# Lightning attention and a two-layer block on one core: the whole program as one list of steps in another order

## The chip, the cores and the metric

The kernel runs on one core of a Trainium2 chip. The metric is the device time of one execution in microseconds (us), lower is better. A core has five engines that take their instructions from queues of their own, each in order: TensorE (PE; PEld is its weight load), VectorE (DVE), ScalarE (ACT), GpSimd (POOL) and SyncE (SP). They wait for one another through semaphores. Transfers between memory and the chip are issued from POOL, SP or ACT.

## The reference, cut to what matters

```
block = 64                       # B, H, S, D = 4, 8, 768, 64
for b in range(S // block):      # 12 blocks of rows, one after the other
    intra = (qb @ kb.T) * Dmask                     # Dmask: lam ** (i - j), causal
    out   = intra @ vb + (qb * lam_pow) @ kv_state
    kv_state = lam_block * kv_state + (kb * rev_pow).T @ vb
x = out, heads side by side      # 3072 x 512
h = x @ w_in                     # 512 x 2048
g = where(h > 0, h, exp(min(h, 0)) - 1)
result = g @ w_out               # 2048 x 512
```

## The kernel before

The 3072 rows are cut into 24 steps s = 0 to 23. A step holds 64 positions of two batches, 128 rows; steps s and s - 2 belong to the same batches, so the state passes from s - 2 to s. Two steps are one group of 256 rows (groups 0 to 11).

Attention. `visit(so, us, ss, sx)` issues the TensorE work of up to four steps at once: the two matmuls of the output of step `so` (from the state, `I`, and from the scores, `O`), the state update `U` of `us`, the scores `S` of `ss`, and the transposes of q and k of `sx`. Around it stand small words on other engines: `C` copies transposed tiles out of PSUM, `P` multiplies scores by the mask (`att_P`, DVE), `V`, `Q` and `D` are the decays of v, q and state (`vd` line 193, `qs` line 220, `sd` line 211; on DVE or POOL, some `sd` on ACT at line 206), `N` forms the new state (line 281), `X` copies the output into `xt` (ACT). From step 10 on, q and k are transposed by a transfer from SP (`dma_T`, two buffers).

First matmul. A unit (`mm1_h`, line 428) fills one PSUM tile `psH` of 128 x 512 with 8 matmuls over 256 rows or 16 over 128; there are two such tiles. `H group.first column.columns.feature` is a unit of groups 0 to 2, `h group.unit` one of the later groups. Exp and Relu run on ACT (`E`), and one DVE instruction joins them into `g` (`G`). In groups 3 and 4 (its first six units) that join reads copies in SBUF; later it reads `psH` itself (lines 472, 474, 475), so the PSUM tile is free only when `g` is done.

Second matmul. Groups 0 to 2 use `mm2` (`M step.feature`, line 495) and copy the sum out (`Z`). From group 3 on a product of 2 x 2 blocks is formed with seven parts (`part`, line 551) instead of eight; four sums `s` of `g` (line 533, DVE), sums of the weights (`B`), kept partial results (`keep`, ACT) and the final adds and stores (`add`, `c2`, `store`) belong to it.

Loads. POOL issues all loads of k, q, v (12 tiles each) and of the weights: `w_in` in four tiles `wi`, each in two halves, `w_out` in four tiles `wo`. The second half of `wi[2]`, and with it all that is behind it on POOL, waits for the semaphore `crossed`, which TensorE raises at the first visit that reads a state (I2).

Order. The queues follow the order in which the program is written. Before, it comes from three places: a hand-placed start of loads (v0, then k, q, v of step 1, w0, those of 2, w1, those of 3, the first half of w2) and `later_loads()`; a list of words `start` for groups 0 to 2; and then a regular loop over groups 3 to 11 and units 0 to 7, in which a visit stands behind the units 1 and 5, a part of the last group's second matmul behind nearly every unit, and sums, adds, decays and loads at fixed units.

Of the kernel before, what the change touches and what calls it, by code (L numbers as in the profile page):

```python
# [16 lines left out]
def kernel(  # L17
# [41 lines left out]

    NB = 12  # L60
# [23 lines left out]
    def load_step(s):  # L84
        load("k", s)
        load("q", s)
        load("v", s)

# [8 lines left out]
    def load_wi(i, halves=range(2)):  # L97

        for c in halves:
            ins = nc.gpsimd.dma_start(  # L100
                out=wi[i][half(c)],
                in_=moe_w_in[c * DM // 2 : (c + 1) * DM // 2, i * WB : (i + 1) * WB].rearrange(
                    "(g p) f -> p g f", p=64
                ),
            )
            if (i, c) == (2, 1):

                ins.wait_op(crossed, 1, "sem-ge")

    def load_wo(i):  # L110
        nc.gpsimd.dma_start(
            out=wo[i][:],
            in_=moe_w_out[i * WB : (i + 1) * WB, :].rearrange("(g p) f -> p g f", p=128),
        )

# [14 lines left out]
    load("v", 0)  # L130
    load_step(1)
    load_wi(0)
    load_step(2)
    load_wi(1)
    load_step(3)
    load_wi(2, [0])

# [325 lines left out]
    def elu(grp, u):  # L463

        psH, nb, T, name = unit[grp, 0, 2, u]
        if grp == 3 or grp == 4 and u < 6:
            mm1_e(grp, 0, 2, u)
            mm1_g(grp, 0, 2, u, NF2)
            return

        r = msb.tile([128, nb, T], FP32, tag="r", bufs=4, name=f"r{name}")
        nc.scalar.activation(r[:], psH[:], AF.Relu, scale=-1.0)  # L472
        e = msb.tile([128, nb, T], FP32, tag="e", bufs=4, name=f"e{name}")
        nc.scalar.activation(e[:], r[:], AF.Exp, scale=-1.0)  # L474
        nc.vector.scalar_tensor_tensor(  # L475
            out=place(grp, 0, 2, u, 2, NF2), in0=e[:], scalar=-1.0, in1=psH[:],
            op0=ALU.add, op1=ALU.max,
        )

    acc = {}  # L480
    nacc = [0]
# [8 lines left out]
    def mm2(s, n0):  # L490
        if n0 == 0:
            acc[s] = M[nacc[0] % 2][:]
            nacc[0] += 1
# [65 lines left out]
    def part(grp, i):  # L559
        d = res.setdefault(grp, dict(A=M[0], B=M[1]))  # L560
        lo, hi = slice(0, HD), slice(HD, DM)
# [6 lines left out]
    def store(s, o, cols, queues=(nc.sync, nc.sync)):  # L568
        for r in range(2):
            queues[r].dma_start(out=rows(s, r)[:, cols], in_=o[half(r), cols])  # L570
# [16 lines left out]
    def c2(grp, queues=(nc.sync, nc.sync)):  # L587
# [5 lines left out]
        store(2 * grp + 1, d[1], slice(0, DM), queues)  # L593
# [12 lines left out]
    def later_loads():  # L606
        load_wi(2, [1])
        load_wo(0)
        load_wi(3)
        load_wo(1)  # L610
        load_wo(2)
        load("k", 4)
        load("q", 4)
        load_wo(3)
        load("v", 4)
        load_step(5)
        load_step(6)
        load_step(7)
        load_step(8)
        load("k", 9)  # L620
        load("q", 9)
        load("k", 10)
        load("q", 10)
        load("v", 9)
        load("k", 11)
        load("q", 11)
        load("v", 10)

    start = (
        "Fq K0 Fk V0 A...0 C0 A.0.. K1 A..0. P0 A...1 N0 C1 A0... X0 V1 A..1. P1 A.1.. A1... X1 "
        "N1 D2 H0.0.1.0 D3 E0.0.1.0 A...2 V2 C2 Q2 H0.1.1.0 A.2.2. I2 R P2 E0.1.1.0 A2... "
        "G0.0.1.0 H0.0.2.4 X2 N2 H1.0.1.0 E0.0.2.4 D4 G0.1.1.0 A...3 G0.0.2.4 E1.0.1.0 C3 V3 "
        "H1.0.1.4 Q3 E1.0.1.4 H0.0.2.6 A.3.3. I3 P3 G1.0.1.0 E0.0.2.6 H0.0.2.10 A3... E0.0.2.10 "
        "H0.0.2.8 X3 G0.0.2.6 G1.0.1.4 E0.0.2.8 H1.0.1.8 N3 D5 M1.0 G0.0.2.10 G0.0.2.8 E1.0.1.8 "
        "H1.1.1.0 M0.0 E1.1.1.0 G1.0.1.8 B1.0 H1.1.1.4 G1.1.1.0 H0.0.2.14 E1.1.1.4 E0.0.2.14 "
        "G1.1.1.4 G0.0.2.14 H1.1.1.8 M1.4 H0.0.2.12 B1.1 E1.1.1.8 E0.0.2.12 M0.4 H1.0.2.12 "
        "G1.1.1.8 G0.0.2.12 M1.8 E1.0.2.12 A...4 H1.0.2.14 C4 G1.0.2.12 M0.8 E1.0.2.14 Q4 A..4. "
        "G1.0.2.14 M1.12 P4 V4 B2.0 M0.12 Z1 M2.0 Z0 A...5 V5 B4.0 M2.4 C5 M3.0 Q5 B2.1 "  # L640
        "A4.4.5.6 M3.4 P5 X4 N4 H2.0.1.12 C6 H2.0.1.4 E2.0.1.12 Q6 M3.8 D6 B4.1 E2.0.1.4 "
        "H2.0.1.8 G2.0.1.12 V6 M3.12 E2.0.1.8 G2.0.1.4 A5.5.6.7 V7 Z3 G2.0.1.8 H2.0.1.0 X5 N5 "
        "H2.1.1.12 E2.0.1.0 P6 M2.8 D7 E2.1.1.12 G2.0.1.0 H2.1.1.4 M2.12 E2.1.1.4 G2.1.1.12 "
        "H2.1.1.0 C7 Z2 G2.1.1.4 A6.6.7.8 E2.1.1.0 Q7 M4.0 N6 X6 G2.1.1.0 M4.4 P7 H2.1.1.8 C8 "
        "M4.8 E2.1.1.8 V8 D8 Q8 A7.7.8.9 T10 G2.1.1.8 M4.12 X7 N7 P8 Z4 C9 B3.0 B3.1 "
    )
    steps = {
        "I": lambda s: visit(s, None, None, None, True), "C": att_C, "P": att_P, "X": lambda s: att_X(s, nc.scalar),
        "Y": lambda s: att_X(s, nc.vector), "N": att_N, "D": lambda s: decay_s(s, eng=nc.vector), "L": load_step,
        "V": lambda s: decay_v(s, nc.vector if s < 99 else nc.gpsimd),  # L650
        "Q": lambda s: decay_q(s, nc.vector if s < 10 else nc.gpsimd),
        "H": mm1_h, "E": mm1_e, "G": mm1_g, "M": mm2, "Z": mm2_o, "K": consts, "B": w_sum, "T": dma_T,
    }
    for word in start.split():
        if word[0] == "A":
            visit(*(int(x) if x else None for x in word[1:].split(".")))
        elif word[0] == "R":
            later_loads()
        elif word[0] == "F":
            cast0(word[1])  # L660
        else:
            steps[word[0]](*(int(x) for x in word[1:].split(".") if x))

    lo, hi = slice(0, HD), slice(HD, DM)

    five = [(3, 2), (3, 4), (3, 6), (4, 0)]
    nload = 12
    for grp in range(3, NG):  # L670
        old, new = grp - 2, grp - 1
        for u in range(8):
            mm1_h(grp, 0, 2, u, NF2)
            s = 2 * grp + 2 + u // 4
            if s < NS and u % 4 == 0:

                if nload < NS:
                    load("k", nload)
                    load("q", nload)
                if nload <= NS:  # L680
                    load("v", nload - 1)
                    nload += 1
            if s < NS and u % 4 == 1:
                if s not in (10, 12):
                    decay_q(s + 1, nc.vector if s < 10 else nc.gpsimd)
                if s not in (10, 11, 12):
                    decay_s(s + 1, eng=nc.vector if s < 10 else nc.gpsimd)
                visit(
                    s, s if s < NS - NPR else None, s + 1 if s + 1 < NS else None,
                    s + 2 if s + 2 < NT else None,  # L690
                )
                dma_T(s + 3)

            if (grp, u) in five:
                mm2(5, 4 * five.index((grp, u)))
            end = grp == NG - 1
            if old >= 3 and u in (0, 2):
                part(old, {0: 3, 2: 7}[u])
            if new >= 3:
                at_u = {1: 2, 3: 4, 4: 1, 5: 5, 6: 6, 7: 3} if end else {3: 2, 4: 1, 5: 4, 6: 5, 7: 6}  # L700
                if u in at_u:
                    part(new, at_u[u])

            if old >= 3 and u == 1:
                add(old, 0, hi, res[old]["A"][:, hi], "p35")
                store(2 * old, res[old][0], slice(0, DM), ((nc.gpsimd if end else nc.sync),) * 2)
            if old >= 3 and u == 0:
                g_sum(old, 3)
            if new >= 3 and u in (4, 5, 6):
                g_sum(new, {4: 1, 5: 2, 6: 4}[u])  # L710
            if end and u == 3:
                g_sum(new, 3)
            if new >= 3 and u == 4:
                add(new, 0, lo, res[new]["A"][:, hi], "p2")
            if s + 1 < NS:
                if u % 4 == 1:
                    att_P(s + 1)
                if u % 4 == 2:
                    att_C(s + 2)
                    att_N(s)  # L720
                if u in (3, 7) and grp > 3:
                    decay_v(s + 1, nc.vector)
                if (grp, u) == (4, 2):
                    decay_q(s + 1, nc.vector)
            if old >= 3 and u == 2:
                c2(old)
            elu(grp, u)
            if (grp, u) == (5, 3):
                decay_q(s + 1, nc.vector)
            if (grp, u) == (4, 4):  # L730
                decay_s(11)
            if (grp, u) in ((5, 2), (5, 4)):
                decay_s(13, range(2) if u == 2 else range(2, NHP))
# [4 lines left out]
            if (grp, u) == (4, 5):  # L738
                decay_s(12)
# [71 lines left out]
```

## Time and profile before

| | |
|---|---|
| runs | 205.8, 208.4, 208.91 us; median 208.4 |
| profiled execution | 204.2 us from the first to the last instruction; its own whole time is not given apart |
| PE, DVE, ACT, POOL busy | 189.6, 168.7, 146.5, 123.4 us |
| instructions | 7590 |
| bytes moved | 24.36 MB, mean 119 GB/s |

A busy time is the sum over an engine's instructions, those that overlap counted once. In the profile a line such as `L428` is the kernel's line, `out<-in` the tiles, `x16` a count of instructions, and a bracket names how long the engine was idle before an instruction and what released it. A slow release may be put down to a wrong engine where several were waited for.

### The profile page before, as it was taken

What the parts mean: (1) busy time and instruction counts of PE and PEld (TensorE: products, weight loads), DVE (VectorE), ACT (ScalarE), POOL (GpSimd) and SP (SyncE); (2) the same over time, 40 slices, a digit from 0 to 9 for tenths busy, and PEclk for the clock granted to TensorE, in tenths of its full rate; (3) what the DMA queues carried; (4) which work ended last, traced back from release to release, by engine and by line L of the source; (5) the groups of instructions that cost most, each with busy time, mean ns of one, the idle gap of its engine ahead of it and who ended that gap; (6) DMA issues with size and microseconds to landing.
All of it is one profiled execution on the core that took longest, in us unless ns stands there. A gap on an engine that the chain in (4) does not pass through costs nothing.

```text
span 204.2 us, 7590 instructions
## 1 busy us (share of the span) xinstructions
PE 189.6 (93%) x3216; PEld 156.6 (77%) x3216; DVE 168.7 (83%) x279; ACT 146.5 (72%) x283; POOL 123.4 (60%) x174
## 2 busy tenths in 40 slices
PE   0679899999999999999999989999999999999991
PEld 0457777647777777888888878888888888888881
DVE  4776996489989998999989999989979866758672
ACT  5626987635774879999878677788688788876820
POOL 8977832598998959997709999999222200020000
PEclk9999999999999999999999999999999999999998
DMA  6999999999999999999999999999915404004043
GB/s 102 157 171 171 152 206 196 180 124 156 117 148 150 173 108 172 153 134 78 74 163 109 206 105 86 185 111 105 169 27 69 94 0 108 0 6 100 3 103 103
DMA packets 94194, 24.36 MB, mean 119 GB/s; under 512 B 86160, under 2 KB 91152, under 8 KB 94160
## 3 DMA queue, kind: packets, MB, share of 16 engines
q0 software_dynamic: 73744, 13.64, 94.7%
q1 hardware_dynamic: 19968, 9.77, 26.9%
q10 hardware_dynamic: 448, 0.46, 1.0%
q8 instruction: 25, 0.41, 0.9%
q14 instruction: 9, 0.07, 0.1%
HBM read 27.27 MB, written 6.29 MB: 164 GB/s over the span
## 4 chain that ended last, share of the span: by engine, by line
PE 85%; DVE 4%; DMA 3%; POOL 3%; issue 2%; ACT 1%; POOLq 0%; DVEq 0%
PE psH L428 40%; PE psM L551 23%; PE psM L495 10%; DMA wi<-in_moe_w_in_dram 3%; PE psO_None L328 2%; POOL vn L79 1%; PE psZ L352 1%; PE psO_None L337 1%; PE psHB L551 1%; PE psHA L551 1%; DVE s L533 1%; PE psZ L344 1%; DVE g L475 1%; POOL kn L79 1%; PE psO L359 1%
## 5 line engine op out<-in xcount | busy, mean ns | idle before, releaser
L428 PE MATMUL psH<-xt,wi 128*128 128x256 f16 (+1 forms) x896 | 100.1, 261 | 1.9 <-ACT e L438 0.6
L428 PEld LDWEIGHTS <-wi 128*128 128x128 f16 x896 | 78.2, 100 | 13.3 <-issue 2.1
L475 DVE SCALAR_TENSOR_TENSOR g<-e,psH 128x512 f16<-128x512 f32 x58 | 39.6, 683 | 14.3 <-ACT e L474 13.8
L472 ACT ACTIVATE r<-psH 128x512 f32<-128x512 f32 x58 | 34.7, 598 | 18.3 <-PE psH L428 18.2
L474 ACT ACTIVATE e<-r 128x512 f32<-128x512 f32 x58 | 36.5, 630 | 1.8
L79 POOL DMA_DIRECT2D kn<-in_k_dram x46 | 32.2, 720 | 9.2 <-DMA wo<-in_moe_w_out_dram 5.1
L79 POOL DMA_DIRECT2D vn<-in_v_dram x48 | 34.1, 741 | 2.0 <-DMA wi<-in_moe_w_in_dram 1.1
L438 ACT ACTIVATE e<-psH 128x512 f32<-128x512 f32 x38 | 22.8, 601 | 14.7 <-PE psH L428 14.4
L551 PEld LDWEIGHTS <-s 128*128 128x128 f16 x288 | 28.1, 98 | 3.3
L445 DVE SCALAR_TENSOR_TENSOR g<-e,r 128x512 f16<-128x512 f32 x38 | 25.7, 685 | 4.1 <-ACT r L440 4.0
L220 POOL TENSOR_TENSOR qs<-TD,powi 128x512 f16<-128x512 f16 x11 | 13.9, 1264 | 19.3 <-PE psO_None L328 13.1
L79 POOL DMA_DIRECT2D qn<-in_q_dram x36 | 25.3, 735 | 0.0
L551 PE MATMUL psM<-wt,s 128*128 128x256 f16 x192 | 24.9, 273 | 0.0
L495 PE MATMUL psM<-wo,g 128*128 128x512 f16 x96 | 24.0, 379 | 0.0
L440 ACT ACTIVATE r<-psH 128x512 f16<-128x512 f32 x38 | 22.9, 602 | 0.0
L551 PEld LDWEIGHTS <-g 128*128 128x128 f16 x216 | 20.6, 98 | 2.6
L193 DVE TENSOR_TENSOR vd<-vn,rev 128x512 f16<-128x512 f16 x22 | 17.2, 783 | 1.8 <-DMA vn<-in_v_dram 1.7
L228 DVE TENSOR_TENSOR P<-psZ,mask 128x512 f16<-128x512 f32 x24 | 16.4, 684 | 2.0 <-PE psZ L344 1.1
L551 PE MATMUL psM<-wo,g 128*128 128x256 f16 x136 | 17.6, 272 | 0.0
L495 PEld LDWEIGHTS <-g 128*128 128x128 f16 x96 | 8.7, 98 | 7.0
L570 POOL DMA_DIRECT2D out_dram<-o x2 | 1.1, 574 | 21.1 <-DVE o L585 21.1
L533 DVE TENSOR_TENSOR s<-g 128x1024 f16<-128x1024 f16 x18 | 13.8, 764 | 0.0
(85 smaller groups left out, 228.7 us busy)
## 6 DMA issues: line engine op xcount, KB each, us to landing
out_dram<-o SPq DMA_DIRECT2D x43, 128.0 KB, 3.3
vn<-in_v_dram POOLq DMA_DIRECT2D x48, 64.0 KB, 5.0
kn<-in_k_dram POOLq DMA_DIRECT2D x46, 64.0 KB, 4.3
qn<-in_q_dram POOLq DMA_DIRECT2D x36, 64.0 KB, 4.5
wi<-in_moe_w_in_dram POOLq DMA_DIRECT2D x8, 256.0 KB, 8.9
wo<-in_moe_w_out_dram POOLq DMA_DIRECT2D x4, 512.0 KB, 12.6
qn<-in_q_dram POOLq DMA_DIRECT2D x5, 128.0 KB, 5.3
kraw<-in_k_dram SPq DMA_DIRECT2D x2, 128.0 KB, 4.7
```

Of the source, the lines that this page charges most:

```text
L79: nc.gpsimd.dma_start(out=keep[s][half(r)], in_=src[b + r, :, c * L : (c + 1) * L, :].rearrange("h p d -> p h d"),)
L193: eng.tensor_tensor(out=st[s]["vd"][:], in0=vn[s][:], in1=rev[:].unsqueeze(2).broadcast_to([128, H, D]), op=ALU.mult,)
L228: nc.vector.tensor_tensor(out=d["P"][:].rearrange("p y j t -> p y (j t)"), in0=psS, in1=mask[:].rearrange("p y j t -> p y (j t)"), op=ALU. ...
L428: nc.tensor.matmul(psH[:, i, :], lhsT=wi[n // 4][:, kk, (n % 4) * 128 : (n % 4 + 1) * 128], rhs=xt[grp][:, kk, c0 * 128 : c0 * 128 + T], s ...
L438: nc.scalar.activation(e[:], psH[:], AF.Exp)
L440: nc.scalar.activation(r[:], psH[:], AF.Relu)
L445: nc.vector.scalar_tensor_tensor(out=place(grp, c0, nc_, n0, nb, step), in0=e[:], scalar=-1.0, in1=r[:], op0=ALU.add, op1=ALU.min,)
L472: nc.scalar.activation(r[:], psH[:], AF.Relu, scale=-1.0)
L474: nc.scalar.activation(e[:], r[:], AF.Exp, scale=-1.0)
L475: nc.vector.scalar_tensor_tensor(out=place(grp, 0, 2, u, 2, NF2), in0=e[:], scalar=-1.0, in1=psH[:], op0=ALU.add, op1=ALU.max,)
L495: nc.tensor.matmul(acc[s], lhsT=g_of(s, n), rhs=wo[n // 4][:, n % 4, :], start=(n == 0), stop=(n == NFT - 1),)
L551: nc.tensor.matmul(to, lhsT=lhsT, rhs=rhs, start=start and n == 0, stop=stop and n == NF2 - 1, skip_group_check=True,)
```

## The change

The whole order, loads and loop included, becomes one list `plan`, read word by word. `start`, `later_loads()` and the loop are gone; each former loop statement is now a word (`h`, `e`, `g`, `p` part, `s` sum, `k` keep, `a` add, `c`, `o` store, `d` decay on ACT, and a trailing `.1` puts a decay on POOL). Each engine has the same instructions as before, each as often, in another order. The wait on `crossed` before the second half of `wi[2]` is gone. The bank of each of the first six `mm2` sums is a table.

```
+    plan = (
+        "lv1 Fq Fk A...0 C0 A..0. lv0 K0 P0 A0... V1 lq2 lq1 lk1 lk2 w0.0 w0.1 lv2 w1.1 A...1 K1 "
+        "w1.0 lv3 lq3 lk3 V0 C1 A.0.. N0 D2 A...2 w2.1 w2.0 A..1. P1 A.1.. N1 A1... X0 H0.0.1.0 "
+        "X1 C2 y0 w3.1 lq4 Q2 lk4 V2 E0.0.1.0 w3.0 H0.1.1.0 E0.1.1.0 A.2.2. P2 I2 A2... X2 N2 "
+        "G0.0.1.0 H0.0.2.4 H1.0.1.0 A...3 y1 E0.0.2.4 G0.1.1.0 V3 D4 E1.0.1.0 H1.0.1.4 y2 D3 C3 "
+        "H0.0.2.6 Q3 G1.0.1.0 E1.0.1.4 I3 A.3.3. H0.0.2.10 P3 G1.0.1.4 y3 E0.0.2.6 A3... N3 "
+        "G0.0.2.6 G0.0.2.4 E0.0.2.10 H0.0.2.8 lv4 H1.0.1.8 M0.0 G0.0.2.10 X3 H1.1.1.4 E0.0.2.8 "
+        "E1.0.1.8 G1.0.1.8 E1.1.1.4 H1.1.1.8 E1.1.1.8 A...4 H1.1.1.0 lq5 lq6 lk5 E1.1.1.0 "
+        "H0.0.2.14 E0.0.2.14 G0.0.2.8 M1.0 H1.0.2.12 E1.0.2.12 M1.4 H0.0.2.12 G1.1.1.8 D5 "
+        "G0.0.2.14 B1.0 B2.0 E0.0.2.12 G0.0.2.12 C4 H1.0.2.14 lv5 B1.1 G1.1.1.4 M0.4 M1.8 A..4. "
...
+        "G2.1.1.0 h3.3 e3.1 Q9 e3.0 lv10 A8.8.9. lk12 M4.12 e3.4 lq13 D9 T12 N8 g3.1 P9 h3.2 "
+        "lk14 lv12 lk13 V9 lv13 h3.7 e3.3 B4.1 g3.4 Z3 M5.0 g3.0 X8 g3.3 e3.2 A9.9.10. P10 h3.5 "
+        "h3.6 M5.4 Q10 M5.8 N9 e3.7 X9 lq14 h4.3 e3.5 g3.7 V10 e3.6 h4.2 Q11 A10.10.11. Q12.1 "
+        "lk17 lv19 M5.12 T13 h4.0 h4.1 d11.0.4 Z4 g3.2 g3.5 lk15 V11 lk20 lq17 D10 e4.3 e4.2 X10 "
...
+        "g7.6 P18 e7.7 g7.7 k6.p35 a6.0 e8.0 A18.18.19. X18 h8.1 e8.1 p6.7 h8.2 o12.0 P19 s7.1 "
+        "g8.0 p7.2 N18 h8.3 lk21 g8.1 e8.2 A19.19.20. D19.1 h8.4 e8.3 k7.p2 c6 g8.2 p7.1 h8.5 "
...
+        "k10.c45 s10.4 p10.6 e11.6 k10.u2 g11.5 h11.7 p10.3 g11.6 p10.7 a10.2 e11.7 g11.7 o20.0 "
+        "s11.1 j p11.1 p11.4 p11.5 o19.0 o17.0 s11.2 s11.4 s11.3 k11.u1 p11.6 c10 k11.u2 o21.0 "
+        "p11.2 a11.3 o22.1 p11.7 k11.c45 c11 o23.3 p11.3 a11.2 o22.2 "
+    )
...
-    def load_step(s):
...
-    def load_wi(i, halves=range(2)):
-        for c in halves:
-            ins = nc.gpsimd.dma_start(
...
-            if (i, c) == (2, 1):
-                ins.wait_op(crossed, 1, "sem-ge")
+    def load_wi(i, c):
+        nc.gpsimd.dma_start(
...
+    loads = {
+        "l": lambda a: load(a[0], int(a[1:])), "w": lambda a: load_wi(*map(int, a.split("."))),
+        "y": lambda a: load_wo(int(a)),
+    }
...
-    load("v", 0)
-    load_step(1)
-    load_wi(0)
-    load_step(2)
-    load_wi(1)
-    load_step(3)
-    load_wi(2, [0])
...
+    BANK = (1, 0, 0, 1, 0, 1)
...
-    def later_loads():
-        load_wi(2, [1])
-        load_wo(0)
-        load_wi(3)
-        load_wo(1)
-        load_wo(2)
-        load("k", 4)
-        load("q", 4)
-        load_wo(3)
-        load("v", 4)
-        load_step(5)
...
-    for grp in range(3, NG):
-        old, new = grp - 2, grp - 1
-        for u in range(8):
-            mm1_h(grp, 0, 2, u, NF2)
...
+    steps = {
...
+        "K": consts, "B": w_sum, "T": dma_T, "h": lambda g, u: mm1_h(g, 0, 2, u, NF2), "e": elu_e,
+        "g": elu_g, "s": g_sum, "p": part_of, "a": sums, "c": c2, "o": store,
     }
+    for word in plan.split():
...
+        elif word[0] in loads:
+            loads[word[0]](word[1:])
```

## The prediction

> **What bounds the kernel now.** I read the page first, then stretches of the span by engine, then the chain that ended last and the timelines of the places where TensorE stands still.
>
> ```profile
> PE 189.6 (93%) x3216; PEld 156.6 (77%) x3216; DVE 168.7 (83%) x279; ACT 146.5 (72%) x283; POOL 123.4 (60%) x174
> PE 85%; DVE 4%; DMA 3%; POOL 3%; issue 2%; ACT 1%; POOLq 0%; DVEq 0%
> ```
> ```profile
> 0.00:13.24 13.24, 4.64 (x136) 3.51 (x137) 8.34 (x23) 6.93 (x20) 11.15 (x22) 1.00 1.27 138
> 13.24:34.00 20.76, 19.34 (x345) 16.29 (x346) 16.04 (x28) 14.69 (x29) 12.63 (x19) 1.00 1.34 181
> 34.00:112.00 78.00, 78.00 (x1473) 60.33 (x1472) 70.98 (x116) 59.02 (x117) 62.83 (x91) 1.00 1.76 137
> 112.00:126.00 14.00, 13.47 (x236) 11.48 (x235) 13.67 (x20) 10.67 (x20) 14.00 (x18) 1.00 1.52 133
> 126.00:204.20 78.20, 74.11 (x1031) 64.96 (x1029) 59.65 (x97) 55.16 (x100) 22.74 (x27) 0.99 0.63 80
> ```
> The second fence has a stretch, its length, and the busy time of PE, PEld, DVE, ACT and POOL. TensorE is the bound: from 34 to 112 us it never stops, and after 126 only a tail of 4.1 us is missing. It is idle 8.6 us before the first unit of the first matmul (word H), 1.4 us up to 34, 0.5 around 118, and in the tail. The change moves no work to another engine, so it can win only in these four places and lose anywhere.
>
> **The start.** The rows are GpSimd's load issues (start, duration), then the chain from w0 on, then a later H.
>
> ```profile
> 1.41 1.54 POOL L79 DMA_DIRECT2D vn<-in_v_dram  x2 [0.15 <-issue]
> 7.01 0.71 POOL L100 DMA_DIRECT2D wi<-in_moe_w_in_dram  x1 [0.20 <-issue]
> 7.71 1.38 POOL L79 DMA_DIRECT2D kn<-in_k_dram  x2
> 9.05 0.56 POOL L76 DMA_DIRECT2D qn<-in_q_dram  x1
> ```
> ```profile
> 7.01 6.18 DMA wi<-in_moe_w_in_dram
> 13.24 1.89 PE psH L428 x16
> 15.13 0.57 PE psM L398 x9
> 15.70 0.54 PE psM L403 x4
> 16.24 1.71 PE psH L428 x16
> 18.45 0.70 DVE P L228
> ...
> 29.11 0.89 PE psH L428 x16
> ```
> The first H waits for the second half of w0: issued at 7.01, 6.18 us to land, start at 13.24. In the new list k2 and q2 stand ahead of w0, 1.38 + 0.56 = 1.94 us more of issuing, so w0 lands near 15.2. There is a second way to be late. Ahead of H now also stands step 2's transpose (A...2), and k2's second half goes out near 7.7. The next rows are the landing times of k1's loads and of k2's in the old order.
>
> ```profile
> DMA to landing us min/median/max: 4.8/4.9/5.0
> DMA to landing us min/median/max: 5.6/5.8/6.0
> ```
> With 5.0 to 6.0 us, then the transpose (0.54) and S, P and O of step 1 (about 1.5 together), that chain ends between 14.7 and 15.7. I take 15.4 for the first H: +2.2, bounds +1.5 and +3.0. In return step 2's transpose no longer stands between the first two H: 0.57 + 0.54 = -1.1. K0 and V0 now run on VectorE after the first casts instead of in its wait for them; I cost that at nothing, as they end long before k2 lands. If k2 were early it would be 1.2 us of VectorE, and P0 would be late next.
>
> The first two H took 1.89 and 1.71 us, the same 16 matmuls 0.89 us at 29.11. So TensorE begins at half speed and reaches full speed about 4.6 us after it became dense, although the granted clock reads 1.00 there. The sum lets this repeat. The Trainium skill ("TensorE: Matmul & The Clock Gate", part 1) says that the clock opens after a busy window of about 3.4 us and that the windows run free of the kernel's start. The trace agrees with the order of it (4.6 us); by that rule the instant is a matter of phase, and denser work before the first H can open it a window sooner, which is the faster rival.
>
> **The removed wait and the weights.**
>
> ```profile
> 16.69 0.64 POOL L100 DMA_DIRECT2D wi<-in_moe_w_in_dram  x1
> 18.81 0.61 POOL L100 DMA_DIRECT2D wi<-in_moe_w_in_dram  x1 [1.48 <-PE psO_None L328]
> 24.93 1.03 PE L428 MATMUL psH<-xt,wi 128*128 128x256 f16 x8 [0.63 <-ACT e L438]
> 25.12 0.54 POOL L76 DMA_DIRECT2D qn<-in_q_dram  x1 [0.84 <-DMA wi<-in_moe_w_in_dram]
> 32.94 1.05 PE L428 MATMUL psH<-xt,wi 128*128 128x128 f16 x16 [0.30 <-ACT r L440]
> wi<-in_moe_w_in_dram POOLq DMA_DIRECT2D x8, 256.0 KB, 8.9
> wo<-in_moe_w_out_dram POOLq DMA_DIRECT2D x4, 512.0 KB, 12.6
> ```
> The second half of w2 was held 1.48 us for `crossed` and landed 6.2 us after its issue, just before 25.12, where a load that waited for it goes on. H0.0.2.10, its first reader, began at 24.93 after 0.63 idle; the releaser named had long ended, so I read this wait as w2's. In the new list nothing holds w2: behind v3, q3 and k3 its halves go out near 16.6 and 17.5 and land by 24, while the reader comes near 25.5. So -0.6, bounds -0.6 and 0 (the median half of wi took 8.9 us). The units that follow press ScalarE as before, but a transpose (A...4, 0.7 us) now stands among them and gives it that time: the 0.30 goes, -0.3. By the same count w3 and wo1 go out 0.7 and 2.2 us later, w3 near 21.5 and wo1 near 23.6; with 8.9 and 12.6 us they land near 30.4 and 36.2, their readers come near 33 and 35.6: 0, at worst +1.
>
> **The steady part.** A unit's buffer is free again when its g on VectorE is done, and TensorE meets it two units later.
>
> ```profile
> 99.14 0.87 PE psH L428 x8
> 100.70 0.98 PE psM L551 x8
> 93.14 0.60 ACT L472 ACTIVATE r<-psH 128x512 f32<-128x512 f32 x1 [0.23 <-PE psH L428]
> 93.77 0.63 ACT L474 ACTIVATE e<-r 128x512 f32<-128x512 f32 x1
> L533 DVE TENSOR_TENSOR s<-g x18: 678/684/1649, 84.0 to 196.3; 128x1024 f16<-128x1024 f16 x18
> 114.83 1.03 POOL L211 TENSOR_TENSOR sd<-st,lamL 128x512 f32<-128x512 f16 x1
> 114.90 1.51 DVE L533 TENSOR_TENSOR s<-s,g 128x1024 f16<-128x1024 f16 x1
> 120.08 1.58 DVE L193 TENSOR_TENSOR vd<-vn,rev 128x512 f16<-128x512 f16 x1
> 121.00 1.55 POOL L211 TENSOR_TENSOR sd<-st,lamL 128x512 f32<-128x512 f16 x1
> 120.20 1.03 PE L428 MATMUL psH<-xt,wi 128*128 128x256 f16 x8 [0.33 <-DVE g L475]
> ```
> A visit costs 0.69 + 0.11 = 0.8 us (gap at 100, and 0.98 for 0.87). The tightest spacing in both orders is visit, unit, part: 0.8 + 0.87 + 0.87 = 2.5 us from a unit's end to the reuse. Of the new list, "h8.0 ... A18 ... h8.1 p6.7 h8.2" is one: VectorE does P19, s7.1 and g8.0 in between, 0.45 + 3 x 0.6 (0.68 each, overlapping) = 2.25 us; r and e (0.60 and 0.63) are over before that. It fits with 0.25 us. The old loop has this place too (s, P, g at the sixth unit of a group), and that is the one that stalled at 118: a sum s took 1.51 instead of 0.68 us beside GpSimd's decay at 114.83, and vd 1.58 beside the one at 121.0. I count this stall as half gone, -0.3 (bounds -0.5, and the slower rival). The Trainium skill ("SBUF — State Buffer", two separate sides) says that a VectorE instruction with two SBUF inputs and a GpSimd one exclude each other on a shared port pair for their whole length. The rows agree in size: 1.51 is about the sum of 0.68 and what was left of the 1.03.
>
> On GpSimd's queue qs12 now stands ahead of k17, v19, k20, q17 and k15, and waits for a transposed tile; these loads serve visits 14 and later, over 20 us on, so 0, and k15 would be late next. On SyncE each transpose stands behind the release of its slot as before.
>
> **The tail.** The stores of tiles 19 and 17 now go out just before 21's.
>
> ```profile
> 126.81 2.46 SPq L570 DMA_DIRECT2D out_dram<-o  x4
> 200.22 0.42 DVE o L585
> ```
> They are four issues of 0.62 = 2.5 us on SyncE, and from about 194.8 end near 197.3; 21's two end at 198.5, before tile 22 exists. +0.1, at worst +1.
>
> **Sum.** 204.2 + 2.2 - 1.1 - 0.6 - 0.3 - 0.3 + 0.1 = 204.2 us of span: no change. The runs of before are 205.8, 208.4 and 208.9, so 1.6 to 4.7 us lie around or beside this span; their mean, 207.7, is 3.5 above it. I predict 204.2 + 3.5 = 207.7 us, where the median of 208.4 is the mark. Its own range, by the bounds (-1.2 to +3.0), is 206 to 211.
>
> **The rivals.**
> Slower: VectorE and GpSimd meet at the tight places. Before, GpSimd's 19 decays (11 qs, 8 sd) cost TensorE only 0.5 us. A hit costs VectorE about 0.8 us, less 0.25 of margin 0.55 for TensorE. From about eight decays that each hit an s or a vd ahead of such a g it decides: 8 x 0.55 = 4.4 us, with no other gain 204.2 + 2.2 - 1.1 + 4.4 + 3.5 = 213.2. For it: the new order puts visits and parts in clusters. Against it: 78 us without a stop in the old order under the same load.
> Faster: full clock from the first H. Both H then take 0.9, saving 0.99 + 0.81 = 1.8, and the transfers keep the chain at the lower bound (0.7 sooner): 204.2 - 2.5 = 201.7, and with the 1.6 of the quickest run 203.3. For it: transposes and visits fill 10 to 15 us. Against it: idle gaps remain there.
> Later clock: it opens a window later, the units up to 20 us stay slow: +2, and wo1 late +1: 210.7, still within 2%.
> That the order is not what the list says, or that loads wait as before: 208.4.
>
> **How the numbers follow.** The forecast has 0.40, the later clock 0.06, no effect 0.02, the slower rival 0.28, the faster one 0.24. So faster by over 2% is 0.24, within 2% 0.48, slower by over 2% 0.28; 2% (4.2 us) is about what a measurement of this kernel can tell from no change. The range takes in most of both rivals: 203.0 to 213.0.
>
> **What would show it.** Right: the first H near 15.4 with step 2's transpose ahead of it, no idle at H0.0.2.10, TensorE unbroken from about 34 us to the last part, the same tail. Wrong: idle of TensorE before units with g as releaser and VectorE instructions of 1.3 us or more ahead of them (slower rival); 0.9 us for the first H (faster rival); a stop at M1.4 or at a visit that waits for a load or a transposed tile.

## The result and the profile after

The changed kernel takes 213.8 us (median of four runs, 211.0 to 215.9), the kernel before, beside it, 207.5: 3.0% longer, 95% interval 2.1 to 4.0%. A second series (a_again below) gave 3.2% (2.2 to 4.3). The forecast was 207.7, no change. The profiled execution took 214.18 us, its span 212.4; it is one of two runs of the four that count as slow (over 1.5% above the fastest), and the two others (211.0 and 213.3) are by the medians 2.7% longer than the three fast ones of before (205.8, 206.6 and 208.4).

The busy line and the chain line of the page:

```profile
PE 191.7 (90%) x3216; PEld 156.5 (74%) x3216; DVE 169.0 (80%) x279; ACT 146.3 (69%) x283; POOL 123.5 (58%) x174
PE 72%; DVE 9%; issue 4%; ACT 2%; DVEq 0%
```

No engine has more to do: the same counts, nearly the same busy time. The chain tells the difference: TensorE fell from 85% to 72% of it, VectorE rose from 4% to 9%, "issue" (waiting for nothing that the profile shows) from 2% to 4%. The stretches, with the old bounds (PE, PEld, DVE, ACT, POOL busy, then clock, DMA, GB/s):

```profile
0.00:13.24 13.24, 4.92 (x124) 3.78 (x125) 7.49 (x21) 6.42 (x19) 12.21 (x24) 1.00 1.23 132
13.24:34.00 20.76, 18.15 (x378) 15.54 (x367) 14.85 (x26) 14.04 (x27) 12.23 (x19) 1.00 1.42 177
34.00:112.00 78.00, 74.61 (x1360) 56.48 (x1358) 67.82 (x111) 55.00 (x110) 60.59 (x87) 1.00 1.75 134
112.00:126.00 14.00, 13.72 (x237) 11.50 (x236) 12.82 (x19) 11.47 (x21) 12.47 (x15) 1.00 1.27 130
126.00:212.40 86.40, 80.29 (x1135) 69.16 (x1133) 66.07 (x106) 59.36 (x107) 25.95 (x31) 1.00 0.62 78
```

From 34 to 112 us TensorE, which had not stopped there, is idle 3.4 us. Stretches of time hold different work in two orders, so I also count by work: the start time of matmul 564, and the time from there to matmul 1832 and from 1832 to the last of the 3216, counted from 0 and taken from the trace's records. (The old order has its first two matmul stages in the first 564 and reaches group 6 at matmul 1832.) The row "changed, 2nd" is the profile of a_again, the changed kernel run once more, at 212.32 us.

```
              at 564   to 1832     to the last
before        42.68      62.33       94.82
changed       44.06      66.24       97.79      +1.4  +3.9  +3.0
changed, 2nd  43.43      64.69       98.04      +0.8  +2.4  +3.2
```

So there are three losses, of different sizes. First TensorE's rows in the start, with the idle time and its releaser in brackets, and one row of GpSimd's load issues:

```profile
15.16 3.57 PE L469 MATMUL psH<-xt,wi 128*128 128x128 f16 x32 [0.36 <-DMA wi<-in_moe_w_in_dram]
20.10 0.32 PE L378 MATMUL psO_None<-P,vn 64*64 64x64 f16 x16 [0.38 <-DVE P L269]
23.07 0.38 PE L444 MATMUL psM<-ident,kn 128*128 128x128 f16 x4 [0.40 <-DMA kn<-in_k_dram]
26.05 1.03 PE L469 MATMUL psH<-xt,wi 128*128 128x256 f16 x8 [0.39 <-ACT e L479]
```
```profile
18.50 0.62 POOL L146 DMA_DIRECT2D wi<-in_moe_w_in_dram  x1 [1.19 <-DMA wi<-in_moe_w_in_dram]
```

The first H starts at 15.16, for w0, and the first two H take 3.57 us, again at half speed. A new stop for k3 stands at 23.07, and the w2 stop is still there, at 26.05 (the `e` named as its releaser is a wrong one: w2's last packets landed at 25.96). Then the middle:

```profile
52.95 0.45 PE L469 MATMUL psH<-xt,wi 128*128 128x128 f16 x5 [0.27 <-issue]
56.95 1.57 PE L469 MATMUL psH<-xt,wi 128*128 128x128 f16 x25 [0.34 <-issue]
61.77 0.68 PE L469 MATMUL psH<-xt,wi 128*128 128x128 f16 x9 [1.80 <-issue]
67.14 0.21 PE L400 MATMUL psO<-ident,qn 64*64 64x64 f16 x1 [0.29 <-issue]
```

These stops, 2.7 us together, are a kind that the profile before does not have. They fall inside a unit or a transpose, between matmuls with the same operands, where no buffer and no semaphore is due. And the late part, with VectorE and GpSimd around two of the stops and VectorE before the third:

```profile
125.71 1.05 PE L599 MATMUL psM<-wo,s 128*128 128x256 f16 x8 [0.28 <-DVE s L581]
141.50 1.05 PE L599 MATMUL psM<-wo,s 128*128 128x256 f16 x8 [0.55 <-DVE s L581]
150.00 1.03 PE L469 MATMUL psH<-xt,wi 128*128 128x256 f16 x8 [0.56 <-DVE g L524]
158.31 1.03 PE L469 MATMUL psH<-xt,wi 128*128 128x256 f16 x8 [0.29 <-DVE g L524]
159.97 1.03 PE L469 MATMUL psH<-xt,wi 128*128 128x256 f16 x8 [0.63 <-DVE g L524]
```
```profile
135.87 1.07 POOL L252 TENSOR_TENSOR sd<-st,lamL 128x512 f32<-128x512 f16 x1
135.93 1.57 DVE L581 TENSOR_TENSOR s<-s,g 128x1024 f16<-128x1024 f16 x1
...
138.26 1.19 POOL L261 TENSOR_TENSOR qs<-TD,powi 128x512 f16<-128x512 f16 x1
...
138.62 1.62 DVE L581 TENSOR_TENSOR s<-g 128x1024 f16<-128x1024 f16 x1
...
148.66 0.69 DVE L640 TENSOR_TENSOR o<-psM,c 128x512 f32<-128x512 f32 x1 [1.56 <-DMA out_dram<-o]
```

Two sums of 0.68 us take 1.6 beside a decay of GpSimd, then TensorE waits for a sum at 141.50; and at 148.66 VectorE has stood 1.56 us for an output store to land, with a g queued behind, for which TensorE waits until 150.00. The tail is as before: 4.0 us from TensorE's last matmul to the end.

### The profile page after: what moved, and what is told of

Read it like the earlier page. It is cut to its first block, busy times and chain, and to the rows that moved or that the text cites. A ratio compares the mean times of both kernels' runs of the same rounds, so it can differ in the third digit from the quotient of the medians.

```text
span 212.4 us, 7591 instructions
## 1 busy us (share of the span) xinstructions
PE 191.7 (90%) x3216; PEld 156.5 (74%) x3216; DVE 169.0 (80%) x279; ACT 146.3 (69%) x283; POOL 123.5 (58%) x174
## 4 chain that ended last, share of the span: by engine, by line
PE 72%; DVE 9%; issue 4%; ACT 2%; DVEq 0%
PE psH L469 34%; PE psM L599 20%; PE psM L543 9%; DVE s L581 3%; DVE g L524 2%; PE psO_None L369 2%; PE psHB L599 1%; PE psHA L599 1%; PE psZ L393 1%; PE psO_None L378 1%; PE psZ L385 1%; DVE vd L234 1%; DVE st L322 1%; DVE o L636 1%; PE psO L400 1%
## 5 line engine op out<-in xcount | busy, mean ns | idle before, releaser
L132 POOL DMA_DIRECT2D vn<-in_v_dram x48 | 33.6, 720 | 4.0 <-DMA kn<-in_k_dram 1.4
L261 POOL TENSOR_TENSOR qs<-TD,powi 128x512 f16<-128x512 f16 x11 | 14.0, 1270 | 28.4 <-DMA TD<-qn 15.4
L486 DVE SCALAR_TENSOR_TENSOR g<-e,r 128x512 f16<-128x512 f32 x38 | 25.0, 685 | 4.8 <-ACT r L481 4.8
L543 PE MATMUL psM<-wo,g 128*128 128x512 f16 x96 | 23.4, 380 | 0.0
L599 PEld LDWEIGHTS <-g 128*128 128x128 f16 x216 | 21.0, 98 | 2.6
L599 PE MATMUL psM<-wo,g 128*128 128x256 f16 x136 | 17.5, 273 | 0.0
L543 PEld LDWEIGHTS <-g 128*128 128x128 f16 x96 | 8.8, 98 | 7.9
L581 DVE TENSOR_TENSOR s<-g 128x1024 f16<-128x1024 f16 x18 | 14.3, 797 | 0.1
L322 DVE TENSOR_TENSOR st<-psZ,sd 128x512 f16<-128x512 f32 x20 | 13.6, 682 | 0.9 <-PE psZ L385 0.9
```

What stands on the lines that cost most here:

```text
L132: nc.gpsimd.dma_start(out=keep[s][half(r)], in_=src[b + r, :, c * L : (c + 1) * L, :].rearrange("h p d -> p h d"),)
L486: nc.vector.scalar_tensor_tensor(out=place(grp, c0, nc_, n0, nb, step), in0=e[:], scalar=-1.0, in1=r[:], op0=ALU.add, op1=ALU.min,)
L543: nc.tensor.matmul(acc[s], lhsT=g_of(s, n), rhs=wo[n // 4][:, n % 4, :], start=(n == 0), stop=(n == NFT - 1),)
L581: nc.vector.tensor_tensor(out=gs[grp, i][:], in0=a, in1=b, op=ALU.add if i == 1 else ALU.subtract)
L599: nc.tensor.matmul(to, lhsT=lhsT, rhs=rhs, start=start and n == 0, stop=stop and n == NF2 - 1, skip_group_check=True,)
```

## The experiments

Ratios are to the kernel before, run beside each group (its medians there: 205.6, 205.2, 205.6 and 205.1 us). Helper line numbers of the test kernels lie a few lines from the changed kernel's. The first four expectations count from 207.5 for before, so compare them as differences.

**Which part of the order costs.** Four kernels are the changed program with its list replaced by mixtures. The cuts lie in the old order ahead of `Z1 M2.0` and ahead of `h6.0`; each section holds the same words in either order.

```
 m_old:    old | old | old        (the old order as a list, without the wait on crossed)
 m_start:  new | old | old
 m_mid:    old | new | old
 m_late:   old | old | new
```

> The list of words, but in the order in which the kernel before issues them, and so without its wait on `crossed`. Theory (the order alone costs the time): 207 us, that is the 207.5 of before less at most the 0.6 of the w2 stop, and no stop of TensorE between 34 and 112 us. Rival (the list as such, or the loads freed of the wait, costs it): nearer the 213.8 of the changed kernel.

> New order up to the last matmul of the second stage (H0, H1, M0, M1), old order behind it. Theory (three separate losses: about 1 us at the start, 3 to 4 us between 34 and 84 us, 3 us between 120 and 160 us): 208.5 us, first H near 15.2, no mid-unit stop. Rival (the start shifts everything behind it and causes the later stops): 211 to 214.

> New order only from the second H2 stage to the end of group 5, old order around it. Theory: TensorE stops inside units at multiples of 128 matmuls between 45 and 70 us, 2 to 3 us together, so 210 to 211 us. Rival (these stops were chance, or came from the late start): 207 to 208, no such stop.

> New order only from group 6 on. Theory: idle of TensorE ahead of units that wait for a g, behind long sums and decays on VectorE, 2 to 3 us between 115 and 160 us, so 210 to 211 us. Rival (VectorE was only late there because of what came before): 207 to 208.

m_old: 205.8 us, ratio 0.9996 (0.996 to 1.004). Neither the list nor the missing wait changes the time. Matmul 564 starts 0.8 us sooner (41.88), with a stop of 0.48 us for a q at 37 us already in that; one of 0.46 for a q at 46 us, and 63.66 us to matmul 1832 instead of 62.33, take it back. m_mid: 208.4, ratio 1.013 (1.006 to 1.020). m_late: 209.0, ratio 1.018 (1.009 to 1.027), and its last part takes 97.67 us for 94.8, as in the changed kernel. So the middle and late losses each appear alone, with nothing of the rest of the new order around them; m_mid shows one of the four stops inside units, the largest. One row of m_mid, three of m_late, and m_late's row of VectorE ahead of the third:

```profile
58.87 0.68 PE L466 MATMUL psH<-xt,wi 128*128 128x128 f16 x9 [1.25 <-issue]
```
```profile
119.64 1.05 PE L596 MATMUL psM<-wo,s 128*128 128x256 f16 x8 [0.63 <-DVE s L578]
135.42 1.05 PE L596 MATMUL psM<-wo,s 128*128 128x256 f16 x8 [0.55 <-DVE s L578]
144.46 1.03 PE L466 MATMUL psH<-xt,wi 128*128 128x256 f16 x8 [1.09 <-DVE g L521]
143.12 0.69 DVE L637 TENSOR_TENSOR o<-psM,c 128x512 f32<-128x512 f32 x1 [2.09 <-PE psZ L390]
```

m_start missed: 214.5, ratio 1.042 (1.035 to 1.049), worse than the whole. VectorE's row and TensorE's at that place, and the stretches from the stop on (columns as above; the granted clock is the third from the end):

```profile
61.58 0.69 DVE L231 TENSOR_TENSOR vd<-vn,rev 128x512 f16<-128x512 f16 x1 [5.37 <-DMA vn<-in_v_dram]
66.53 0.32 PE L366 MATMUL psO<-qs,st 64*64 64x64 f16 x8 [4.64 <-DVE T L283]
```
```profile
62.00:66.50 4.50, 0.00 (x0) 0.00 (x0) 4.50 (x9) 1.08 (x2) 4.50 (x8) 0.81 1.60 143
66.50:70.00 3.50, 3.47 (x101) 2.10 (x101) 3.50 (x7) 0.59 (x1) 2.32 (x4) 0.50 1.95 132
70.00:72.00 2.00, 2.00 (x14) 1.11 (x13) 1.88 (x4) 0.00 (x0) 1.61 (x4) 0.59 2.69 142
72.00:74.00 2.00, 2.00 (x90) 1.34 (x88) 0.30 (x1) 1.08 (x2) 2.00 (x4) 1.00 1.73 107
```

The mixture itself made this: the new order of loads met the old order of visits, the v of step 7 came late, TensorE stood 4.64 us, and the clock fell to 0.50 and came back only near 72 us. It says nothing on the start, so I repeated it with the later loads in the old order:

```
-... lv4 ... lq5 lq6 lk5 ... lv5 ... lk6 lq7 lk7 lq8 ... lv6 lk8 lk10 lk9 lq9 lv7 ...
+... lv4 lk5 lq5 lv5 lk6 lq6 lv6 lk7 lq7 lv7 lk8 lq8 lv8 lk9 lq9 lk10 lq10 lv9 lk11 lq11 lv10
```

> As m_start (new order up to the last matmul of the second stage, old order behind it), but the k, q and v loads of steps 5 to 11 in the old order. Theory (m_start stood 4.6 us at 62 us for the v of step 7, which the new order of loads puts behind the k of steps 8 and 9, and the clock fell for it; the start itself costs 1 us): no such stop, 207 us. Rival (the start itself costs what m_start cost): 212 or more.

207.6 us, ratio 1.011 (1.005 to 1.016): the 4.6 us stop is gone, and this start costs about 1%. Its profile (209.76 us, 2.2 above the median) has a 1.55 us stop for k4 at 33.50 that neither profile of the changed kernel has, and reaches matmul 564 at 45.66, so 1% is more than the start costs in the changed kernel. The three parts then add up to 4.2%, where the whole has 3.0 to 3.2.

**The stops inside units.** The page lists the fetches of instructions as a DMA queue of its own:

```profile
q8 instruction: 25, 0.41, 0.9%
```

25 fetches of 16 KB. The stops lie a multiple of 128 matmuls apart, and 128 matmuls with their weight loads are 256 instructions; 25 times 256 is 6400, and TensorE has 6432 of these two kinds. From the trace's records of this queue (number of the matmul behind the stop, end of the last fetch, start of that matmul, difference, idle time):

```
changed    731   51.51   52.95   1.43   0.27
           859   55.54   56.95   1.40   0.34
           987   60.07   61.77   1.71   1.80
          1115   65.67   67.14   1.47   0.29
2nd        987   58.33   59.88   1.55   1.49
m_mid      987   57.45   58.87   1.41   1.25
```

TensorE goes on 1.4 to 1.7 us after a fetch landed, each time. All five profiles with the new order in the middle and all its matmuls (these three, and a_decays and s_old below) have the stop at 987, of 1.25 to 2.35 us; none of the nine with the old order there has one of 0.2 us. The theory: a block is fetched only when the one before it is begun, and a visit has up to 96 matmuls (the one from 58.45 to 59.41 us), so visits close together use up a block before the next has landed; one block took 4.0 to 5.4 us here, stop included. I tested it from both sides, by adding matmuls to the old order and by leaving some out of the new one.

```
-        if ss is not None:
+        for _ in range(0 if ss is None else 4 if ss in (6, 7, 8) else 1):     # f_rep, old order
             run(mm_S, range(NHP))
```

> Old order (as m_old), with the 16 S matmuls of the visits of steps 6, 7 and 8 issued four times: 144 more matmuls of 64 x 64 between 50 and 65 us, some 1.1 us of TensorE by their spacing in the old trace. Theory (TensorE's instructions come in blocks of 256, that is 128 matmuls with their weight loads, one block ahead, and a block cannot be used before 1.4 us after its fetch landed): new stops in the middle of units, each at a multiple of 128 matmuls and about 1.4 us after a fetch landed, 1.5 to 4 us together: 208.5 to 211. Rival (the stops of the changed kernel come from something else, such as loads or a buffer): 206.5 to 207, no stop there.

```profile
52.57 0.25 PE L375 MATMUL psO<-P,vn 64*64 64x64 f16 x5 [0.36 <-issue]
61.95 1.25 PE L540 MATMUL psM<-wo,g 128*128 128x512 f16 x5 [1.07 <-issue]
66.77 0.28 PE L375 MATMUL psO<-P,vn 64*64 64x64 f16 x9 [0.82 <-issue]
72.15 0.72 PE L466 MATMUL psH<-xt,wi 128*128 128x256 f16 x5 [1.03 <-issue]
```
```
f_rep      859   51.08   52.57   1.49   0.36
          1115   60.46   61.95   1.48   1.07
          1243   65.28   66.77   1.49   0.82
          1371   70.58   72.15   1.57   1.03
```

210.7 us, ratio 1.028 (1.023 to 1.033). Four stops, 3.3 us, at the predicted kind of place, 1.5 to 1.6 us behind a landing; in m_old there is one, of 0.32. The other side:

```
-        if ss is not None:
+        if ss is not None and ss not in (6, 7, 8):            # f_less, new order
             run(mm_S, range(NHP))
-        if us is not None:
+        if us is not None and us not in (5, 6, 7):
             run(mm_U, range(NHP))
```

> The changed kernel once more, beside the next three. Theory: 3% over before again, with the stops of TensorE at multiples of 128 matmuls near 53, 57, 62 and 67 us (2 to 3 us together), and idle ahead of units for s and g between 125 and 160 us (2 us). Rival (the 1.8 us stop at 62 us was chance): under 2% over before, no stop over 0.5 us before 70 us.

> The changed kernel without the S matmuls of steps 6, 7, 8 and the U matmuls of steps 5, 6, 7 (96 of its 3216 matmuls, some 0.7 us of TensorE; the rest then works on old values). Theory (TensorE outruns its blocks of instructions there): the stops between 50 and 70 us shrink from 2.7 us to under 0.7, and with the work left out the kernel is 2.5 to 3 us faster than a_again. Rival (loads or buffers stop it): the stops stay, 0.7 us faster.

a_again: 212.5 us, ratio 1.032 (1.022 to 1.043). The stop of 1.49 us is there, at the same matmul 987; the three small ones are not, so the size of this loss changes from run to run. f_less: 209.3, ratio 1.012 (0.998 to 1.026), 3.2 us less than a_again by the medians, though the two intervals overlap a little. Its only row between 45 and 75 us with idle time is one for ScalarE's copy xt:

```profile
66.18 1.91 PE L466 MATMUL psH<-xt,wi 128*128 128x256 f16 x16 [0.61 <-ACT xt L307]
```

Its matmuls from 564 to 1832 (the 96 left out counted off) take 63.0 us, 3.2 less than the profiled changed kernel and 1.7 less than its second profile. Some 0.7 us of that is the work left out, so 2.5 and 1.0 are left for the stops.

**The late part.** Two edits of m_late, one for each of the waits seen there.

```
 l_stores:   -c4 p5.4 ... h9.4 o15.0 o9.0 T23 k8.p2 o11.0
             +c4 o9.0 p5.4 ... c5 o11.0 ... h9.4 o15.0 T23 k8.p2
 l_decays:   +n = 8 if eng is nc.gpsimd else D        (and L for qs)
             -out=st[s]["sd"][:], ...
             +out=st[s]["sd"][:, :, :, :n], ...        (qs likewise; their buffers made fixed ones)
```

> As m_late, with the stores of output tiles 9 and 11 issued right behind the sums that finish them. Theory (the late stores hold two of the four output buffers, so the sum c6 waits 2.1 us on VectorE for a store to land and the unit behind it 1.1 us for its g): both waits go, 1 us less than m_late, some 207.5; the stops near 119 and 135 us stay. Rival (VectorE is simply too full there): the stop near 144 us stays or moves, 208.5 to 209.

> As m_late, but GpSimd's decays write only 8 of each 64 columns (the rest of their buffers keeps old values). Theory (the stops near 119 and 135 us come from sums s that run 1.6 to 1.9 us instead of 0.68 beside a decay): no sum over 1 us there, both stops of 0.6 us gone, 1.2 us less than m_late: 207.5. Rival (the order simply asks VectorE for too much at once): sums of 0.68 us, but the stops stay: 208.5 to 209.

l_stores: 207.0 us, ratio 1.012 (1.006 to 1.018) for m_late's 1.018 (1.009 to 1.027). The intervals overlap; the trace tells more. VectorE's wait of 2.1 us and TensorE's 1.09 behind it are gone (so the releaser named for the 2.1 us was a wrong one), and the last part takes 96.24 us instead of 97.67. The collisions stay, partly at other places; two of TensorE's three stops after 100 us:

```profile
134.88 1.05 PE L596 MATMUL psM<-wo,s 128*128 128x256 f16 x8 [0.55 <-DVE s L578]
152.22 1.03 PE L466 MATMUL psH<-xt,wi 128*128 128x256 f16 x8 [0.55 <-DVE g L521]
```

l_decays: 205.3 us, ratio 1.002 (0.999 to 1.006). Two of the sums' three groups (busy, mean ns) in m_late and then in l_decays, and l_decays' only stop of TensorE after 100 us:

```profile
L578 DVE TENSOR_TENSOR s<-g 128x1024 f16<-128x1024 f16 x18 | 13.8, 769 | 0.1
L578 DVE TENSOR_TENSOR s<-s,g 128x1024 f16<-128x1024 f16 x9 | 7.0, 781 | 0.0
```
```profile
L586 DVE TENSOR_TENSOR s<-g 128x1024 f16<-128x1024 f16 x18 | 12.3, 689 | 0.1
L586 DVE TENSOR_TENSOR s<-s,g 128x1024 f16<-128x1024 f16 x9 | 6.1, 683 | 0.0
141.70 1.03 PE L474 MATMUL psH<-xt,wi 128*128 128x256 f16 x8 [0.34 <-DVE g L529]
```

The stops of 0.63 and 0.55 are gone and the last 1384 matmuls take 94.5 us instead of 97.7. The rival (the order alone asks too much of VectorE at once) falls: with sums of 0.69 us the same order runs through. The meetings of sums and decays are the larger part of the late loss, the two late stores the smaller; they overlap, as with the short decays the same late stores cost TensorE only 0.34 us.

**All three on the whole new order.**

```
 a_decays:  new order, decays as in l_decays
 a_all:     new order, decays as in l_decays, matmuls as in f_less, stores as in l_stores
```

> The changed kernel with GpSimd's decays cut to 8 of 64 columns, as in l_decays. Theory (in the last part the meeting of decays and sums is the whole loss): no stop after 110 us but the one for the late store (0.5 us), the last 1384 matmuls take 94.5 to 95.5 us instead of 97.8, 2.5 to 3 us faster than a_again. Rival (VectorE or the clusters): 1 us or less.

> The changed kernel with the two cuts of f_less and a_decays and the early stores of l_stores together. Theory (instruction blocks, meetings and stores are all that was lost behind the start): what is left is the start, 1 to 2 us against before, less the 0.7 us of matmuls left out and the 0.5 us of meetings that before has too: 205.5 to 207.5 where before is 205.5. Rival (something else is lost too): 209 or more.

a_decays: 210.3 us, ratio 1.022 (1.012 to 1.032), 2.2 us less than a_again by the medians, a little under the 2.5 to 3 expected, with intervals that meet. Its last part takes 94.7 us, 3.3 less than a_again's, as the theory had it. Its profile, of a run of 213.45 us, has two stops for instructions in the middle, 1.44 and 2.35 us, at matmuls 859 and 987. a_all: 205.8 us, ratio 1.003 (0.999 to 1.006). By work against before it is 0.9 us later at matmul 564, takes 0.3 more to 1832 (62.64, and some 1.0 more when the 0.7 us of matmuls left out are counted) and 0.75 less behind that (94.07, where l_decays has 94.47). So the three causes explain the loss behind the start but for about 1 us in the middle, of which 0.46 is a wait for xt at 64.81. Its start has two stops of the same kind, 0.86 and 0.63 us at matmuls 222 and 349, 1.4 and 1.3 us behind a landing.

**The start.**

```
 s_old:  the first words up to A.2.2. I2 in the old order, the rest as changed
 b_w0:   old order, lv0 w0.0 w0.1 lk1 lq1 lv1 ...
 b_w0b:  old order, lv0 lk1 lq1 w0.0 w0.1 lv1 ...
```

> The changed kernel, but its first 46 words in the old order (everything up to the first part of step 2's visit, with w0 ahead of k2 and q2, and the first H ahead of step 2's transpose). Theory (the start itself costs 1.4 to 2 us at the 564th matmul: 2 us of a later w0, 1.1 us given back by the transpose, the rest by loads that now land late for k3 and w2): first H near 13.2, the 564th matmul 1 to 2 us sooner than in the changed kernel, and 1 to 1.5 us faster than it. Rival (the start is made good later, where TensorE waits for its instructions and for VectorE anyway): the same time as the changed kernel, 3% over before.

> Old order (as m_old) with both halves of w0 loaded ahead of k1, q1 and v1. Theory (the first H waits for w0 alone: its input is there at 11.3 us, it starts at 12.9): first H 11.5 to 12, 0.5 to 1.4 us faster than before. Rival (the later k1, q1 and v1, 1.4 us each, hold step 1 and with it the units behind): no gain or up to 1 us slower.

> As m_old, with w0 ahead of v1 only (k1 and q1 stay first). Theory: first H 11.5 to 12, v1 still lands by 11.3 us and holds nobody, 0.5 to 1.4 us faster than before. Rival (TensorE is still at half speed there and step 1's work only moves behind): no difference, within 0.4%.

s_old: 210.0 us, ratio 1.021 (1.016 to 1.026) for 1.030 and 1.032. First H at 12.73, matmul 564 at 41.27, 2.2 to 2.8 us sooner than in the changed kernel, more than was expected: the second H ran faster here (1.16 us). Its last matmul starts 1.2 and 3.1 us sooner than in the two profiles of the changed kernel, so the work behind does not take the whole of the start back. b_w0: 1.009 (1.006 to 1.013), b_w0b: 1.008 (1.005 to 1.012): both slower than before, by 1.9 and 1.7 us, which is more than theory or rival had, with the first H at 16.08 and 14.08. In b_w0 TensorE stands for q1, in b_w0b for P of step 1, behind the later v1:

```profile
12.59 0.64 PE L436 MATMUL psM<-ident,qn 128*64 128x64 f16 x16 [3.28 <-DMA qn<-in_q_dram]
```
```profile
13.50 0.43 PE L382 MATMUL psZ<-vd,kn 64*64 64x64 f16 x16 [2.18 <-DVE P L266]
```

In these orders of the first loads, whichever goes first, another is waited for. No version was faster than the kernel before beyond its interval.

## Why the prediction was wrong

**The bound** was read right: TensorE sets the time, the change can win in four places and lose anywhere. It lost in three stretches: the start, whose terms were too small; the middle, which had no term; and the late part, whose term had the wrong sign.

**The start** was right in its mechanism. First H forecast 15.4, measured 15.16; half speed for two H, forecast 3.60 us, measured 3.57; the transposes ahead give 1.1 back: step 2's O came at 20.10 for 19.20, +0.9 where the terms said +1.1. The terms behind it were off. The wait on `crossed` was to be worth 0.6. In m_old, without it, the w2 stop shrank from 0.63 to 0.21; the rest of m_old's lead was there before w2 is read, at step 2's O (18.34 for 19.20), from a first H 0.31 sooner and a faster second one, less the 0.48 of the stop for a q. In the new order of loads only 0.24 of the 0.63 went: GpSimd's queue stood 1.19 us for an earlier load, the later of w2's halves went out at 18.50, not at 17.5, and k3, which had no term, was late by 0.40 (0.62 in the second profile). Together +1.4 and +0.8 in the two profiles instead of the +0.2 of the sum.

**The steady part** is where it failed. The step was "it fits with 0.25 us" and, from it, "I count this stall as half gone, -0.3". I gave the meetings of decays and sums one tight place and took the old order's 78 us without a stop as evidence that they do no harm. Measured, the last part lost 3.0 and 3.2 us, and 3.1 to 3.3 us go with the decays (l_decays, a_decays), 0.35 of which before has too. The slower rival thus named the right mechanism, but its condition was wrong: it counted hits, eight at 0.55. The hits did not grow; vd and the three sums together took 44.9 us of VectorE before and 46.0 after, both against 39.6 in l_decays. In m_late it was even less, 43.3, and its last part lost 2.9 us all the same. So neither the hits nor the order costs this alone. What changed is what lies around a hit; my reading, which no run isolates, is that with two or three visits and the sums close together VectorE has no gap left for the 0.9 us that one costs. The fit was also checked for the wrong wait: it asked only when a `g` frees a unit's buffer, and two of the five late stops (125.71 and 141.50) are parts that wait for the sum `s` they read. The Trainium skill ("SBUF — State Buffer", two separate sides) has the port rule that the prediction cited. The trace agrees: sums of 0.69 us in l_decays, where the decays are short, and of 1.57 and 1.62 beside a decay of full length.

**The stores** were looked at only in the tail (19 and 17, right: no cost). Stores 9 and 11, moved behind 15 by the same list, hold two of the four output buffers, and a sum waited 1.56 us for a store; in l_stores 1.4 us of the late part go with them (97.67 to 96.24).

**The blocks of instructions** had no term at all, and no rival; "TensorE unbroken from about 34 us" is the step that failed there. Of the 3.9 us lost in the middle 2.7 are these stops (1.5 of 2.4 in the second profile), and 0.4 is a wait for ScalarE's xt (68.89 us; 0.65 in the second). The prediction's list of what would prove it wrong had no stop with "issue" as releaser. The profile before had the means: "issue" in the chain, the row of queue q8, and visits of 96 matmuls, three quarters of a block each. The Trainium skill ("Runtime: NRT & Kernel Launch", Instruction fetch mechanics) says that instructions come in 16 KiB blocks of 256, that the sequencer fetches the next while it runs the current one, and that the cost of a block's end is mostly hidden. The trace agrees with the block and the one ahead, and with "mostly" in the old order; in the new one 0.3 to 2.4 us at a block's end are not hidden.

**Around the span** I took 3.5 us, from the mean of runs that were not the profiled one. Time and span of the same run differ by 1.8 us throughout (214.18 and 212.4). By that the forecast would have been 206.0, further off; the error of the sum is 6 to 8 us of span. The bounds of the single terms also add up to -0.9 and +3.3, not to the -1.2 and +3.0 of the sum, which changes nothing here.

**The rivals.** The faster one fell: the first two H took 3.57 and 3.35 us in the two profiles, not 1.8. The later clock and the order that does nothing fell too. The slower one explains at most between a third and a half of the loss (3.0 of 8.3 us in one profile, 3.2 of 6.3 in the other).

What stays open: how much of a fetch's time is due to the loads that fill the DMA queues in the middle. Fetches began 1.2 to 2.7 us behind the block boundary there and landed 1.0 to 1.9 us later; behind 126 us, where 78 GB/s move instead of 134, they still took 0.9 to 1.4 us. A run with quiet queues was not tried. Why the same stop measured 1.25 to 2.35 us in different runs is not settled either.

## What to carry to other kernels

Count TensorE's instructions and not only its time: many short matmuls in a cluster can use up a block of instructions before the next is there (here a visit of 96 in 1 us), and the row to look for is idle time with "issue" inside a run of equal matmuls, always the same number of matmuls apart. A stall that an old order hides is not harmless in a new one: list the slow hits that the old order absorbs, and ask of each new cluster whether it still has the slack. When a list is reordered, follow each buffer to the store or load that frees it, since one late store holds its buffer for the whole distance by which it was moved.

## What was not expected of the hardware

TensorE's instructions come in 16 KB blocks of 128 matmuls with their weight loads, and where TensorE waits for a block, it goes on 1.4 to 1.7 us after the fetch landed, in all ten stops listed above. A stop of 4.64 us at 62 us in m_start cost the clock as well: 0.50 of full speed until near 72 us. And the point at which the start reaches full speed moves: with the same words there, the second H began 2.8 and 2.7 us after the first and took 1.91 us in the kernel before and 1.06 in m_old.
